# Unused products in TensorE's idle time, and an offset of its own for each group of operations: a window attention and two MLPs on one core

## The chip, the core and the metric

The kernel runs on one core of one Trainium2 chip. The core has TensorE (PE in the rows; PEld is its weight load), VectorE (DVE), ScalarE (ACT), GpSimd (POOL) and SyncE (SP, which only issues transfers here). Each engine works off its own instructions in the order in which they stand, and waits at the head of its queue until what an instruction needs is there. The metric is the device time in microseconds (us) of one execution.

## The reference

```python
def _attn_ref(q, k, v):                       # 4 batches, 8 heads, 576 positions, head size 64
    scores = scale * np.matmul(q, k.transpose(0, 1, 3, 2))
    rel = pos[:, None] - pos[None, :]
    bias = slopes[:, None, None] * (-np.abs(rel).astype(np.float32))[None, :, :]
    mask = (rel >= 0) & (rel < window)        # window = 128
    scores = np.where(mask, scores + bias[None], -1000000000.0)
    scores = scores - np.max(scores, axis=-1, keepdims=True)
    attn = np.exp(scores)
    attn = attn / (np.sum(attn, axis=-1, keepdims=True) + 1e-09)
    return np.matmul(attn, v).astype(np.float32)
...
def _moe_ref(x, w_in, w_out):                 # 2304 x 512, d_ff 2048
    h = x @ w_in
    sp = np.where(h > 20.0, h, np.log1p(np.exp(np.minimum(h, 20.0))))
    return ((h * np.tanh(sp)) @ w_out).astype(np.float32)
...
def _moe2_ref(x, w_in, w_out):
    h = x @ w_in
    g = np.where(h > 0.0, h, alpha * (np.exp(np.minimum(h, 0.0)) - 1.0))
    return (g @ w_out).astype(np.float32)
...
    x = np.ascontiguousarray(attn_out.transpose(0, 2, 1, 3)).reshape(B * S, H * D)
    x = _moe_ref(x=x, **moe_kwargs)
    return _moe2_ref(x=x, **moe2_kwargs)
```

So there is an attention in which each query sees itself and the 127 positions before it, then an MLP with the Mish function, then an MLP with ELU. The weights arrive as 64-bit numbers.

## The kernel before

**Products.** Large products run in a 32-bit format of reduced precision (fp32r). To keep accuracy each operand is split into a high and a low part (`xh`, `xl`; `wih`, `wil`; `woh`, `wol`; `gh`, `gl`), and each product is three: high by high, low by high, high by low.

**Weights.** Each of 32 blocks of a weight (16 blocks of `d_ff`, input and output side) goes through `load_weights`: a transfer into `raw`, one DVE operation (line 411), two ACT operations (414, 417), a DVE and a POOL operation (419, 422) that make the 32-bit number `bits`, a copy to the high part (353 on ACT or 354 on DVE) and a subtraction to the low part (363, DVE or POOL).

**Attention.** `unit` computes one pair of heads for one part of one batch: scores on PE (`ps_s`, lines 493 to 503), mask, bias and row minimum on DVE (514, 517), exp on ACT (521), division (537 on DVE, 539 on ACT), a transpose on PE (`ps_t`, 562), a masked copy `pt` (578, 353, 587), the product with `v` (`ps_o`, 613). The first attention (batch 0, eight units) comes first of all, since everything else needs its result or stands behind it.

**First MLP.** The positions are cut into chunks of 512 (one per batch) and one of the tails. `steps` is the list of the pieces of hidden products: chunk 0 in 16 steps of two blocks by 256 positions, the later chunks in 16 steps of one block by 512 positions (the tails: two blocks by 256). A step is `hidden1` (24 products of 256 columns, or 12 of 512, into the bank `ph`, line 702), Mish on ACT (709), the split into `gh` and `gl` (353 or 354, and 363), and two steps later `output1` (as many products into `py`, line 730). Steps are counted from 0 here, so step 12 has the 13th Mish. Mish and exp need different tables in ACT, so ACT loads a table (`ACT_TABLE_LOAD`) between attention and Mish. The result goes to DRAM (`ys`, `x_scratch`).

**Second MLP.** Five chunks by 16 steps: `hidden2` (`ph2`, line 843; 12 products of 512 columns), exp, minimum and maximum (851, 852, 854), the split (353, 363), `output2` (872).

**Banks.** PSUM is shared out as two banks each of `h` (`ph`, `ph2`), `y` and `z` (results) and `a` (attention). A hidden step can start only when the split of the step before the last one has read its bank: `gl` frees it.

**The order.** `Plan` collects all operations with their priority (a due time worked out from the numbers in `AT`), and `order()` plays them through with a cost for each: whenever an engine is free, the ready operation with the lowest priority number whose buffers have room is taken and put out next. A copy or a subtraction goes to whichever of two engines would be done with it first. So the numbers in `AT` decide what stands where on every engine. When PE finds nothing, before a planned 80 us and as long as no `z` bank was taken, an unused product is put out:

```python
                    if best is None:
                        if e == "pe" and self.fill and t < self.fill[2] and not self.rings["z"]["next"]:
                            out.append(self.fill[1])
```

It multiplies constant ones, 256 columns of bf16, into a `z` bank that nobody has taken (line 308), and its result is never read.

Of the kernel before, what the change touches and what calls it, by code (L numbers as in the profile page):

```python
# [33 lines left out]
class Buffer:  # L34


    def __init__(self, ring, seq, make):
        self.ring, self.seq, self.make = ring, seq, make
        self.ops, self.real, self.left, self.taken, self.free_at = 0, None, 0, False, None
# [7 lines left out]
class Plan:  # L47
# [6 lines left out]

    WARM = 6.9
# [6 lines left out]
    def __init__(self):  # L62
        self.ops, self.rings, self.last = [], {}, {}
        self.fill, self.early = None, []
# [19 lines left out]
    def op(self, ways, reads=(), writes=(), prio=0.0, moved=0, rows=1.0, table=None, port=False):  # L84
# [20 lines left out]
        self.ops.append(dict(ways=ways, deps=deps, bufs=bufs, prio=prio, moved=moved, rows=rows, table=table, port=port))  # L105

    def order(self):
# [47 lines left out]
        while events:  # L155
# [4 lines left out]
            while again:  # L160
                again = False
                for e, q in waiting.items():
# [26 lines left out]
                    for b in o["bufs"]:  # L189
                        if not b.taken:  # L190
                            b.taken = True
                            b.ring["next"] += 1
                    at = t
# [32 lines left out]
        return out  # L226

# [33 lines left out]
def tile_window_attention_two_mlps(ctx, tc, qkv0, qkv1, qkv2, w1d, w2d, out):  # L261
# [46 lines left out]
    plan.fill = (256 / 2400 + 0.003, lambda: nc.tensor.matmul(unused[:, :256], ones[:, :P], ones[:, :256], start=True, stop=True), AT["fill"])  # L308
# [10 lines left out]
    def buf(tag, shape, dt=F32, name=None):  # L319
# [4 lines left out]
        def make():  # L324
            t = where.tile([P, words], dt, tag=tag, name=name or tag, bufs=slots)
# [8 lines left out]
        x = plan.buffer(tag, slots, make)  # L334
        return x

# [62 lines left out]
    def load_weights(wd, into, f, k, pr, stage):  # L399

        hi, lo = (buf(nm, (DM,), F32R) for nm in (("wih", "wil"), ("woh", "wol"))[k])
        into[f, k] = hi, lo
        for o in range(0, DM, HW):
# [24 lines left out]
                lambda hi=hi, o=o: hi()[:, o:o + HW], [bits] + [(hi, x) for x in parts], [(lo, x) for x in parts], pr + AT["wlo"])  # L428

# [522 lines left out]
```

## Time and profile before

| what | value |
|---|---|
| median of 3 runs | 952.38 us (952.3 to 956.86) |
| time of the profiled execution | 954.04 us |
| span of the profiled execution, first to last instruction | 952.3 us |
| mean granted TensorE clock (1 is full speed) | 0.983 |
| busy: PE, DVE, ACT, POOL | 932.0, 514.6, 505.8, 175.1 us |

The profiler records each instruction's start and length. A busy time is the time in which at least one instruction of the engine runs. PE's lengths hold the whole way of a product through the array, so they overlap, and a busy PE is not PE at its peak. The granted clock is recorded beside it: 1.00 is 2.4 GHz and 0.50 is 1.2 GHz. A wait is put down to the instruction whose end released the waiting one.

### The profile page before, as it was taken

The page shows a single profiled execution, that of the slowest core. Times are in us where ns is not written, and L with a number is a line of the kernel's source. Part 1 is how long each engine was busy: PE and PEld are TensorE (multiplying, and loading weights), DVE is VectorE, ACT ScalarE, POOL GpSimd, SP SyncE. Part 2 cuts the span into 40 slices and gives each one's busy share as a digit, 9 for nine tenths or more (in the row PEclk, how much of TensorE's full clock was granted, in tenths as well). Part 3 has the DMA queues.
Part 4 walks back from the last instruction along what each step waited for, and adds up shares of the span by engine and source line. Part 5 has one row for each costly group of instructions (what it writes and reads, how often), then busy time and mean ns, then how long its engine had stood idle before and what let it go on. Part 6 is the DMA issues. An engine that isn't in the chain of part 4 may idle for free.

```text
span 952.3 us, 13731 instructions
## 1 busy us (share of the span) xinstructions
PE 932.0 (98%) x5061; PEld 775.9 (81%) x5061; DVE 514.6 (54%) x1305; ACT 505.8 (53%) x1022; POOL 175.1 (18%) x153
## 2 busy tenths in 40 slices
PE   9989998999999999999999999999999999999998
PEld 6668987978878777789988878888888888888887
DVE  7776878767623346871477796343334333333333
ACT  5788988785826566882477773233223222322232
POOL 2553454520100001010355552000000000000000
PEclk9789998999999999999999999999999999999999
DMA  8343445233212123440444541011001000100010
GB/s 237 118 134 114 158 156 179 91 121 107 77 35 70 42 59 103 131 138 34 124 157 141 166 154 34 1 45 45 1 0 41 27 1 1 44 1 1 1 45 23
DMA packets 32387, 75.08 MB, mean 79 GB/s; under 512 B 5696, under 2 KB 12352, under 8 KB 32320
## 3 DMA queue, kind: packets, MB, share of 16 engines
q1 hardware_dynamic: 32320, 74.20, 24.7%
q8 instruction: 40, 0.66, 0.3%
q14 instruction: 27, 0.22, 0.1%
HBM read 64.23 MB, written 9.96 MB: 78 GB/s over the span
## 4 chain that ended last, share of the span: by engine, by line
PE 79%; DVE 2%; ACT 1%; DMA 1%; issue 0%; DVEq 0%
PE py L872 21%; PE ph L843 20%; PE py L730 17%; PE ph L702 16%; PE ps_o L613 2%; PE ps_t L562 1%; PE ps_s L496 1%; PE ps_s L498 1%; PE ps_s L503 1%; DMA qkv<-in_qkv_dram 1%; DVE kk L363 0%; DMA x_scratch<-ys 0%; DVE ps_s L514 0%; DVE p L537 0%; DVE gl L363 0%
## 5 line engine op out<-in xcount | busy, mean ns | idle before, releaser
L363 DVE TENSOR_TENSOR gl<-ph,gh 128x512 fp32r<-128x512 f32 (+1 forms) x152 | 100.3, 660 | 168.7 <-ACT gh L353 168.2
L843 PE MATMUL ph<-x,wih 128*128 128x512 f32 (+1 forms) x640 | 181.8, 368 | 2.4 <-DVE gl L363 2.4
L353 ACT ACTIVATE gh<-ph 128x512 fp32r<-128x512 f32 (+1 forms) x143 | 81.6, 572 | 128.6 <-PE py L872 125.1
L843 PEld LDWEIGHTS ph<-x,wih 128*128 128x128 f32 x640 | 117.4, 188 | 25.4 <-DVE gl L363 3.1
L730 PE MATMUL py<-gh,woh 128*128 128x256 f32 (+1 forms) x384 | 136.2, 355 | 1.7 <-ACT gh L353 1.0
L702 PE MATMUL ph<-xh,wih 128*128 128x256 f32 (+1 forms) x384 | 134.5, 350 | 1.3 <-DVE gl L363 1.0
L730 PE MATMUL py<-gh,wol 128*128 128x256 f32 (+1 forms) x384 | 130.4, 340 | 1.0 <-DVE wol L363 0.6
L702 PE MATMUL ph<-xl,wih 128*128 128x256 f32 (+1 forms) x384 | 130.1, 339 | 0.7 <-DVE xl L363 0.7
L730 PE MATMUL py<-gl,woh 128*128 128x256 f32 (+1 forms) x384 | 130.3, 339 | 0.3 <-DVE gl L363 0.3
L702 PE MATMUL ph<-xh,wil 128*128 128x256 f32 (+1 forms) x384 | 130.0, 339 | 0.0
L843 PE MATMUL ph<-x,wil 128*128 128x512 f32 (+1 forms) x320 | 117.7, 368 | 0.0
L851 ACT ACTIVATE e<-ph 128x512 f32<-128x512 f32 (+1 forms) x80 | 44.4, 555 | 133.3 <-PE ph L843 132.4
L872 PE MATMUL py<-woh,gl 128*128 128x512 f32 x288 | 112.3, 390 | 0.0
L872 PE MATMUL py<-woh,gh 128*128 128x512 f32 x288 | 112.3, 390 | 0.0
L872 PE MATMUL py<-wol,gh 128*128 128x512 f32 x288 | 112.1, 389 | 0.0
L422 POOL TENSOR_TENSOR bits<-bits,raw 128x512 int32<-128x512 int32 x64 | 89.1, 1395 | 98.4 <-DVE bits L419 75.0
L852 DVE TENSOR_SCALAR e<-e 128x512 f32<-128x512 f32 (+1 forms) x80 | 34.7, 434 | 112.8 <-ACT e L851 112.5
L702 PEld LDWEIGHTS ph<-xh,wih 128*128 128x128 f32 x384 | 73.4, 191 | 13.0 <-issue 3.3
L730 PEld LDWEIGHTS py<-gh,woh 128*128 128x128 f32 x384 | 73.7, 192 | 10.9 <-issue 1.5
L730 PEld LDWEIGHTS py<-gh,wol 128*128 128x128 f32 x384 | 73.6, 192 | 9.6 <-DVE wol L363 1.0
L702 PEld LDWEIGHTS ph<-xh,wil 128*128 128x128 f32 x384 | 73.5, 192 | 7.8
L702 PEld LDWEIGHTS ph<-xl,wih 128*128 128x128 f32 x384 | 73.6, 192 | 7.6 <-DVE xl L363 0.9
(101 smaller groups left out, 1498.4 us busy)
## 6 DMA issues: line engine op xcount, KB each, us to landing
raw<-in_w_dram SPq DMA_DIRECT2D x64, 512.0 KB, 4.2
qkv<-in_qkv_dram SPq DMA_DIRECT2D x12, 640.0 KB, 4.0
qkv<-in_qkv_dram SPq DMA_DIRECT2D x16, 288.0 KB, 2.9
x_scratch<-ys SPq DMA_DIRECT2D x18, 256.0 KB, 2.2
out_dram<-yo SPq DMA_DIRECT2D x18, 256.0 KB, 2.0
qkv<-in_qkv_dram SPq DMA_DIRECT2D x8, 512.0 KB, 3.6
xr<-x_scratch SPq DMA_DIRECT2D x16, 256.0 KB, 2.8
v<-in_qkv_dram SPq DMA_DIRECT2D x12, 192.0 KB, 2.4
```

The source lines that it names most:

```text
L353: ways = [("act", act_cost(n, sbuf), lambda: nc.scalar.activation(o(), i(), AF.Copy), 0.0), ("dve", dve_cost(n, sbuf), lambda: nc.vector.t ...
L363: both(n, lambda eng: eng.tensor_tensor(out=o(), in0=i(), in1=hi().bitcast(F32), op=ALU.subtract), reads, writes, prio, only, port=not only)
L422: gps(HW, lambda raw=raw, bits=bits: nc.gpsimd.tensor_tensor(out=bits().bitcast(I32), in0=bits().bitcast(I32), in1=raw()[:, :, 0].bitcast( ...
L496: nc.tensor.matmul(o, qh()[:, j, qo:qo + r], kk()[:, j, ks], start=(j == 0), stop=False, skip_group_check=True)
L498: nc.tensor.matmul(o, ql()[:, j, qo:qo + r], kk()[:, j, ks], start=False, stop=True, skip_group_check=True)
L613: nc.tensor.matmul(o()[j * D:(j + 1) * D, c0:c0 + math.prod(y.shape[1:])], vn()[:kr, n, j], y, start=n == 0, stop=n == nkb - 1, skip_group ...
L702: nc.tensor.matmul(ph()[:, i * n:(i + 1) * n], wt()[:, cs], xx()[:, at], start=(c == 0 and m == 0), stop=(c == KC - 1 and m == 2))
L730: nc.tensor.matmul(py()[:, k, :], wt()[:, cs], gg()[:, i * n:(i + 1) * n], start=(f == 0 and a == 0 and k == 0), stop=(f == NF - 1 and a = ...
L843: nc.tensor.matmul(ph(), wt()[:, cs], xx(), start=(c == 0 and m == 0), stop=(c == KC - 1 and m == 2))
L851: act(n, lambda: nc.scalar.activation(e(), ph(), AF.Exp), [ph], [e], t, sbuf=False, table="exp")
L852: dve(n, lambda: nc.vector.tensor_scalar(out=e(), in0=e(), scalar1=1.0, scalar2=-1.0, op0=ALU.min, op1=ALU.add), (), [e], t, fast=True)
L872: nc.tensor.matmul(py(), gg()[:, ts_], wt(), start=(f == 0 and a == 0), stop=(f == NF - 1 and a == 2))
```

## The change

First, PE's idle time takes unused products for longer: up to a planned 170 us instead of 80, and once the `z` banks are in use they go into the bank that the next attention, hidden or output operation will take (`spare`, which names none while PE has lately been busy enough by the planner's own count). That operation starts its bank anew, so it overwrites them. Second, each operation belongs to a group (one step's hidden products, one unit's scores, one block of weights), and the dictionary `SHIFT` adds an offset to the priority of 114 such groups. Third, a few numbers of `AT` differ (`late`, `relt`, `wadd`, `fill`). The new numbers `k0`, `k1`, `u4` and `u5` stand at values that give the steps and start times of before, and the new form of `output1` and `split_x` gives the same products.

```diff
-AT = dict(lag=2, step=6.96, late=23.66, copy=1.19, both=0.34, conv=-34.61, conv1=8.2, mish=-3.26, out=-0.67,
+AT = dict(lag=2, step=6.96, late=25.76, copy=1.19, both=0.34, conv=-34.61, conv1=8.2, mish=-3.26, out=-0.67,
...
-          g=-8.44, stage=-21.52, fill=80.0, u0=0.0, u1=5.67, t0=1.26, t1=11.22, t2=4.45, u2=33.61, u3=4.87,
-          norma=0.5, normp=8.33, relt=-13.66, d00=-2.11, d01=-2.85, d10=0.27, d11=1.21, dx=3.28, plain=6.14,
-          mm2=8.39, first=-1000.0, second=-53.57, wadd=2.54, whi=-10.73, wlo=9.29, norm=-2.13, mask=-3.68, gl=13.52,
-          newton=-9.59, elu=-24.7, lead=1, turn=2.71, held=28.54)
+          g=-8.44, stage=-21.52, fill=170.0, enough=1.5, u0=0.0, u1=5.67, t0=1.26, t1=11.22, t2=4.45, u2=33.61, u3=4.87,
+          norma=0.5, normp=8.33, relt=-15.35, d00=-2.11, d01=-2.85, d10=0.27, d11=1.21, dx=3.28, plain=6.14,
+          mm2=8.39, first=-1000.0, second=-53.57, wadd=1.47, whi=-10.73, wlo=9.29, norm=-2.13, mask=-3.68, gl=13.52,
+          newton=-9.59, elu=-24.7, lead=1, turn=2.71, held=28.54, k0=8, k1=0, u4=0.0, u5=5.67)
+
+SHIFT = dict(H10=18, H11=60.7, H12=6.4, H13=-5.2, H18=-8, H2=-14.4, H4=5.8, H6=-28.2, H68=26.9, H69=44.6, H7=-24.9,
...
+    ENOUGH = AT["enough"]
...
-        self.ops.append(dict(ways=ways, deps=deps, bufs=bufs, prio=prio, moved=moved, rows=rows, table=table, port=port))
+        prio += SHIFT.get(self.group, 0.0)
+        self.ops.append(dict(group=self.group, ways=ways, deps=deps, bufs=bufs, prio=prio, moved=moved, rows=rows, table=table, port=port))
...
-                        if e == "pe" and self.fill and t < self.fill[2] and not self.rings["z"]["next"]:
+                        if e != "pe" or t > self.fill[2]:
+                            continue
+                        if t <= self.WARM or not self.rings["z"]["next"]:
                             out.append(self.fill[1])
-                            free[e] = self.clocked(t, self.fill[0], 1.0)
-                            heapq.heappush(events, free[e])
+                        else:
+                            b = self.spare(q, t)
+                            if b is None:
+                                continue
+                            b.taken = True
+                            b.ring["next"] += b.seq == b.ring["next"]
+                            out.append(lambda b=b: self.fill[3](b))
+                        free[e] = self.clocked(t, self.fill[0], 1.0)
+                        heapq.heappush(events, free[e])
                         continue
...
+    def spare(self, q, t):
+
+        k = int(t / self.TICK)
+        if self.columns.get(k, 0) + self.columns.get(k - 1, 0) * (k + 1 - t / self.TICK) > self.ENOUGH * self.COLUMNS:
+            return None
+        for i in sorted(q, key=lambda i: (self.ops[i]["prio"], i)):
+            bufs = self.ops[i]["bufs"]
+            if all(self.room(b, t) for b in bufs):
+                for b in bufs:
+                    if b.bank and (not b.taken or b.unused):
+                        b.unused = True
+                        return b
+        return None
...
+    unused_product = lambda to: nc.tensor.matmul(to[:, :256], ones[:, :P], ones[:, :256], start=True, stop=True)
+
+    def unused_before(b):
+        b()
+        unused_product(b.whole)
+
+    plan.fill = (256 / 2400 + 0.003, lambda: unused_product(unused), AT["fill"], unused_before)
```

The order of instructions on the engines shows what this moves. The rows below are instructions in the order in which they stand, without times; a number behind a name tells one buffer from another of the same name.

**PE in the first attention.** PE of before, behind the transpose of the third unit's probabilities; a row `LDWEIGHTS` and the `MATMUL unused` behind it are one unused product, and four of them stand here:

```order
L562 MATMUL ps_t_294<-ident_68,p_202 128x128 x2
L493 MATMUL ps_s_302<-qkv_153,qkv_146 128x256 x2
L562 MATMUL ps_t_318<-ident_68,p_257 128x128 x2
L308 LDWEIGHTS const-bfloat16-1.0
L308 MATMUL unused_67<-const-bfloat16-1.0 128x256
...
L493 MATMUL ps_s_336<-qkv_171,qkv_166 128x256 x2
L613 MATMUL ps_o_350<-pt_274,qkv_112 64x256 x2
```

PE of the change at the same place, where thirteen of them stand, and further on, where the first ones stand that go into the bank of a later product (four ahead of the product `ps_o_621`):

```order
L623 MATMUL ps_t_294<-ident_68,p_202 128x128 x2
L554 MATMUL ps_s_301<-qkv_153,qkv_146 128x256 x2
L623 MATMUL ps_t_316<-ident_68,p_202 128x128 x2
L623 MATMUL ps_t_322<-ident_68,p_253 128x128 x2
L351 LDWEIGHTS const-bfloat16-1.0
L351 MATMUL unused_67<-const-bfloat16-1.0 128x256
...
L623 MATMUL ps_t_356<-ident_68,p_253 128x128 x2
...
L351 MATMUL ps_o_621<-const-bfloat16-1.0 128x256
...
L623 MATMUL ps_t_632<-ident_68,p_536 128x128 x2
```

In all there are 82 unused products in place of 53: up to this place 44 in place of 41 (the 29 at the start among them), then 13 in place of 4, 8 in place of 8 before the first hidden products, and behind these 17 in place of none. The real products are the same 4720 in both.

**ACT around the 14th Mish.** ACT of before, from the 13th Mish (step 12, the first row) to the 14th (step 13, the last):

```order
L709 ACTIVATE ph<-ph 128x512
L353 ACTIVATE wih<-bits 128x512
L417 ACTIVATE raw<-raw 128x512
L353 ACTIVATE gh<-ph 128x512
L414 ACTIVATE raw<-raw 128x512
L709 ACTIVATE ph<-ph 128x512
```

ACT of the change between the same two, where 18 instructions and two table loads stand (left out are four of `raw`, one of `woh` and three of `p,st`):

```order
L777 ACTIVATE ph<-ph 128x512
L408 ACTIVATE woh<-bits 128x512
L408 ACTIVATE gh<-ph 128x512
L408 ACTIVATE wih<-bits 128x512
L582 ACT_TABLE_LOAD
L582 ACTIVATE p,st<-p,st 128x128
...
L473 ACTIVATE raw<-raw 128x512
L600 ACTIVATE p<-p,st 128x128 x4
L408 ACTIVATE wih<-bits 128x512
L777 ACT_TABLE_LOAD
L777 ACTIVATE ph<-ph 128x512
```

A unit's exp, four weight blocks' pieces and four divisions of the attention now stand between two steps that followed each other closely. The count of table loads is 71 in both.

**PE where the second MLP begins.** PE of before: half of the first `ph2`, then the last four groups of three `output1` products (`py`), then its other half, the second `ph2` and the third:

```order
L843 MATMUL ph2_5911<-x2_5135,wil_5151 128x512
L730 MATMUL py_5196<-gh_5895,woh_2279 128x512
...
L730 MATMUL py_5233<-gh_5895,wol_2298 128x512
L843 MATMUL ph2_5911<-x2_5155,wih_5137 128x512
...
L843 MATMUL ph2_5911<-x2_5181,wil_5151 128x512
L843 MATMUL ph2_5961<-x2_5125,wih_5190 128x512
...
L843 MATMUL ph2_5961<-x2_5181,wil_5201 128x512
L843 MATMUL ph2_6005<-x2_5125,wih_5248 128x512
```

PE of the change at the same place:

```order
L930 MATMUL ph2_5930<-x2_5154,wih_5166 128x512
...
L930 MATMUL ph2_5930<-x2_5210,wil_5180 128x512
L809 MATMUL py_5225<-gh_5940,woh_2340 128x512
...
L809 MATMUL py_5262<-gh_5940,wol_2351 128x512
L930 MATMUL ph2_5984<-x2_5154,wih_5219 128x512
...
L930 MATMUL ph2_5984<-x2_5210,wil_5230 128x512
L930 MATMUL ph2_6008<-x2_5154,wih_5277 128x512
```

All twelve products of the first `ph2` now stand ahead of the four `py` groups. On DVE two copies of `py` to `ys` stand ahead of the first `ph2`'s minimum where one stood (the other of the two was ACT's).

## Rows read from the trace of the kernel before

**Rows 1.** The page: span, busy time by engine, the clock in 40 slices

```profile
span 952.3 us, 13731 instructions
...
PE 932.0 (98%) x5061; PEld 775.9 (81%) x5061; DVE 514.6 (54%) x1305; ACT 505.8 (53%) x1022; POOL 175.1 (18%) x153
...
PEclk9789998999999999999999999999999999999999
```

**Rows 2.** Windows: PE, PEld, DVE, ACT, POOL busy, clock, DMA, GB/s

```profile
8.00:80.00 72.00, 65.46 (x378) 47.81 (x378) 56.13 (x206) 58.58 (x166) 33.58 (x41) 0.83 0.54 164
80.00:120.00 40.00, 39.81 (x319) 37.09 (x318) 30.70 (x80) 34.47 (x72) 16.85 (x12) 1.00 0.42 130
...
170.00:240.00 70.00, 69.39 (x426) 57.85 (x424) 51.53 (x159) 53.05 (x110) 20.07 (x14) 1.00 0.33 101
...
549.00:564.00 15.00, 12.64 (x56) 10.10 (x56) 13.74 (x17) 12.38 (x22) 9.69 (x8) 1.00 0.66 206
```

**Rows 3.** Windows, the same columns: the four stretches at half clock

```profile
19.30:29.50 10.20, 10.20 (x39) 5.71 (x38) 5.84 (x26) 5.87 (x22) 3.42 (x5) 0.50 0.82 273
43.20:53.40 10.20, 9.56 (x42) 7.19 (x41) 10.10 (x32) 8.99 (x23) 7.80 (x11) 0.50 0.42 135
70.50:73.90 3.40, 3.40 (x16) 2.47 (x17) 3.35 (x14) 3.39 (x11) 1.74 (x2) 0.50 0.60 204
155.80:162.70 6.90, 6.40 (x32) 5.21 (x32) 6.76 (x24) 6.61 (x17) 2.65 (x3) 0.51 0.61 203
```

**Rows 4.** Windows, the same columns: what stands just ahead of those

```profile
16.00:19.30 3.30, 2.18 (x12) 1.40 (x12) 2.32 (x13) 2.87 (x11) 0.75 (x2) 1.00 1.07 292
39.80:43.20 3.40, 2.02 (x10) 1.19 (x9) 2.63 (x12) 2.66 (x10) 1.09 (x2) 1.00 0.28 77
67.00:70.50 3.50, 2.05 (x10) 1.43 (x11) 2.34 (x7) 2.64 (x5) 1.14 (x2) 1.00 0.47 122
152.40:155.80 3.40, 1.25 (x8) 0.82 (x7) 3.37 (x10) 3.39 (x6) 2.51 (x2) 1.00 0.66 219
```

**Rows 5.** Windows of line L308 alone (PE, PEld): unused products

```profile
19.30:29.50 10.20, 2.10 (x8) 1.04 (x8) 0.50 0.82 273
```

**Rows 6.** Waits of PE, 8 to 240 us: three of 16 rows

```profile
PE ps_t L562 <- DVE p L537: 1.7, 2, 1.4
...
PE ps_s L493 <- DMA qkv<-in_qkv_dram: 0.8, 1, 0.8
...
PE ps_s L503 <- DVE st L517: 0.2, 1, 0.2
```

**Rows 7.** Windows, the columns of group 2

```profile
145.00:163.00 18.00, 14.29 (x93) 11.93 (x92) 17.25 (x51) 16.75 (x37) 6.76 (x6) 0.81 0.58 197
```

**Rows 8.** ACT's timeline around the 13th and 14th Mish (line L709)

```profile
152.07 1.28 ACT L709 ACT_TABLE_LOAD   x1
153.37 0.58 ACT L709 ACTIVATE ph<-ph 128x512 f32<-128x512 f32 x1
...
155.99 0.60 ACT L709 ACTIVATE ph<-ph 128x512 f32<-128x512 f32 x1
```

**Rows 9.** Instructions of ACT up to 240 us: busy, mean ns

```profile
L539 ACT ACTIVATE p<-p,st 128x128 f32<-128x128 f32 x20 | 6.9, 392 | 0.0
```

**Rows 10.** Chain in order of time: start, length, products

```profile
169.58 1.44 PE py L730 x12
...
886.37 3.40 PE py L872 x15
```

**Rows 11.** PE's timeline where the second MLP begins

```profile
554.71 0.39 PE L843 MATMUL ph<-x,wil 128*128 128x512 f32 x1
...
557.43 0.39 PE L843 MATMUL ph<-x,wil 128*128 128x512 f32 x1
560.18 0.73 PE L843 MATMUL ph<-x,wih 128*128 128x512 f32 x2 [2.36 <-DVE gl L363]
```

**Rows 12.** DVE's timeline at the same place

```profile
559.45 0.68 DVE L363 TENSOR_TENSOR gl<-ph,gh 128x512 fp32r<-128x512 f32 x1
```

More of the change, by code (lines that the diff above doesn't have):

```diff
@@ L38, in __init__ @@
         self.ring, self.seq, self.make = ring, seq, make
-        self.ops, self.real, self.left, self.taken, self.free_at = 0, None, 0, False, None
+        self.real, self.left, self.taken, self.free_at = None, 0, False, None
+        self.bank, self.unused = False, False
     def __call__(self):
@@ L192, in order @@
                             b.ring["next"] += 1
+                        b.unused = False
                     at = t
@@ L324, in make @@
         def make():
-            t = where.tile([P, words], dt, tag=tag, name=name or tag, bufs=slots)
+            t = x.whole = where.tile([P, words], dt, tag=tag, name=name or tag, bufs=slots)
             n = math.prod(shape)
@@ L334, in buf, with grouped @@
         x = plan.buffer(tag, slots, make)
+        x.bank = where is psum
         return x
+    def grouped(name, fn, *a):
+        plan.group = name
+        fn(*a)
+        plan.group = None
     def act(n, emit, reads, writes, prio, sbuf=True, extra=0, table=None):
@@ L442, in unit @@
         tp = t0 + AT["prep"] * dt
+        me = f"u{b}{part}{pr}"
+        plan.group = me + "l"
         cut = [sum(W[:i]) for i in range(4)]
@@ L666, in operands, with split_x @@
         x_of[ci] = [(buf(f"xh{c}", (C2,), F32R), buf(f"xl{c}", (C2,), F32R)) for c in range(KC)]
-    def split_x(ci, t):
-        need = [(b, 2) for b in range(B)] if ci == B else [(ci, 0), (ci, 1)]
+    def split_x(ci, t, only=None):
+        need = [(b, 2) for b in range(B)] if ci == B else [(ci, x) for x in range(2) if only in (None, x)]
         if any((*x, pr) not in ended for x in need for pr in range(NPAIR)):
@@ L673, in split_x @@
         parts = range(n // C1)
+        if only is not None:
+            parts, n = [only], C1
+        at = slice(parts[0] * C1, parts[0] * C1 + n)
         if ci == B:
@@ L716, in output1 @@
         n = C2 // len(fs)
-        if fs[0] == 0:
-            py_of[ci, half] = [buf(tag, (C2 // n, n), name="py") for tag in ("yyzz" if n == C2 else "zz" if half else "yy")]
-        ys_of = py_of[ci, half]
+        if (ci, half) not in py_of:
+            if ci in (0, B):
+                py_of[ci, half] = [(buf("yz"[half], (2, C1), name="py"), half, (2 * y, 2 * y + 1)) for y in range(2)]
+            else:
+                py_of[ci, 0] = py_of[ci, 1] = [(buf(tag, (1, C2), name="py"), None, (y,)) for y, tag in enumerate("yyzz")]
@@ L720, in output1, with mm @@
         gh, gl = g_of.pop(s)
+        targets = py_of[ci, half] if n == C1 else [x for h in range(2) if ci == 0 or not h for x in py_of[ci, h]]
         for i, f in enumerate(fs):
             woh, wol = w1[f, 1]
-            w = C2 // n
-            for y, py in enumerate(ys_of):
-                def mm(i=i, f=f, y=y, py=py, woh=woh, wol=wol):
-                    for k in range(w):
-                        cs = slice((w * y + k) * P, (w * y + k + 1) * P)
+            for y, (py, only, cols) in enumerate(targets):
+                g0 = i * n if n == C1 else C1 * (only or 0)
+                o0 = half * C1 if only is None else 0
+                m = C1 if n == C1 or only is not None else C2
+                first = (ci, py) not in begun
+                begun.add((ci, py))
+                def mm(f=f, py=py, woh=woh, wol=wol, cols=cols, g0=g0, o0=o0, m=m, first=first):
+                    for k, c in enumerate(cols):
+                        cs = slice(c * P, (c + 1) * P)
@@ L788, in tile_window_attention_two_mlps @@
             if fs[0] == 0 and ci > 0:
-                at(t - 0.2, split_x, ci, t + AT["split"])
+                at(t - 0.2, grouped, f"x{ci}{steps[s][2]}", split_x, ci, t + AT["split"], steps[s][2] if ci == 1 and K1 else None)
             at(t, hidden1, s, t)
```

74 lines of the change are left out of this document (53 added, 21 removed).

## The prediction

> **What bounds the kernel now.** I read the page first. PE is busy 932.0 of 952.3 us [rows 1], so the time is PE's work plus what PE loses to waits and to the lower clock, and only those losses can change: the real products are the same 4720. The clock line of the page shows where the lower clock lies: as a 7 or an 8 in three of the first seven slices, 0 to 167 us, and nowhere behind [rows 1]. The windows then cut the span by how PE does. From 80 to 120 us and from 170 to 240 us PE is busy 39.81 of 40 and 69.39 of 70 us at clock 1.00 [rows 2], so there nothing is lost. Losses are in 8 to 80 us (mean clock 0.83), around 145 to 163 us (clock 0.81, PE busy 14.29 of 18) [rows 2, 7], and 2.4 us of waiting in 549 to 564 us [rows 2].
>
> The windows at half clock say what the clock costs. PE is busy 10.20, 9.56, 3.40 and 6.40 us in them [rows 3]; at 1.2 GHz that is work of half the time, so 5.1, 4.8, 1.7 and 3.2 us are lost at most. What the reader is to see beside it is who else is full. In the first stretch DVE and ACT work 5.84 and 5.87 of 10.20 us: there everybody waits for PE. In the others DVE works 10.10 of 10.20, 3.35 of 3.40 and 6.76 of 6.90 us, and ACT nearly as much [rows 3]: there a faster PE would soon wait for them. Just ahead of each stretch PE was thinly busy: 2.18 of 3.30, 2.02 of 3.40, 2.05 of 3.50 and 1.25 of 3.40 us [rows 4]. The waits of PE are many and small: 16 rows that add up to 12.6 us, no single one over 1.4 us [rows 6].
>
> **The change, part by part.** The sum is made against the profiled span, 952.3 us. That execution took 954.04 us as a whole, 1.7 more; the median of the runs is 952.38, so the span and the median agree within 0.1 us, and I apply the sum to the median.
>
> *The unused products themselves.* There are 29 more. Eight of them take 2.10 us at half clock [rows 5], 0.26 each, so the added ones cost from nothing (if each lies in idle time of PE) to 7.6 us (if none does). The order puts thirteen where before has four behind the third unit's transpose, and the later ones ahead of attention products and hidden products near the places of [rows 4]; PE is idle 1.1 to 2.2 us in each of those windows. Thirteen at 0.13 (full clock) are 1.7 us against 1.1 idle there, so a little is not hidden: I take +0.5.
>
> *The first stretch at half clock.* Of its 10.20 busy us, 2.10 are unused products [rows 5], so real work is 8.1 us at half speed and 4.05 us could be won if the clock stayed up. DVE and ACT can follow, with 4.3 us idle each. The hole that stands ahead of it (1.12 us of 3.30) is what the thirteen products fill. It is not sure that the clock stays for all of it, since the same attention has few products per microsecond either way. From 0 to -4.0; I take two thirds, -2.7.
>
> *The second and third stretch.* Up to (9.56 + 3.40) / 2 = 6.5 us of PE's time, but DVE is full in both [rows 3], so nearly all of it would come back as waits for DVE or ACT. From 0 to -6.5; I take -1.0, near the lower end, since the row says that DVE has 0.15 us left of 13.6.
>
> *145 to 163 us.* PE is idle 18 - 14.29 = 3.7 us there [rows 7] and loses 3.2 to the clock, 6.9 in all, because DVE (17.25) and ACT (16.75) are full for all 18. They are much less full later (51.53 and 53.05 of 70 us from 170 to 240 us, [rows 2]), so it is a peak of work that can be moved. The order gives PE more to do meanwhile. Between the last hidden product of step 14 and the first output product that reads its result stand 52 products in before and 99 in the change; for step 15 it is 45 and 89, for step 16 29 and 67. They hold 24 hidden products of the next chunk, of 512 columns, which before has behind. At 0.12 us for 256 columns (1.44 for 12) and 0.227 for 512 (3.40 for 15) [rows 10], the cover of step 14 goes from about 6 to about 14 us. Against it stands ACT: see the rival below. From -6.9 to +4.7 (the rival's); I take -2.5.
>
> *More work on ACT.* Up to the 25th Mish the change puts on ACT five more divisions, three more copies out of `ps_o`, two more of weights, one more each of `q`, `kk` and `pt` and one fewer of `gh`, twelve more in all, which DVE did before. A division is 0.39 us [rows 9]; twelve such are 4.7 us. ACT works 34.47 of 40 us from 80 to 120 us [rows 2], so it has room, but not everywhere. From 0 to +4.7; I take +1.0.
>
> *The other waits.* Of the 12.6 us [rows 6] some 9 lie outside 145 to 163 us. The offsets shift all of them, in both directions. SP's transfers are the same, and some stand a few places earlier or later in its queue; of PE's waits 0.8 us end on a transfer [rows 6], so I price that move at nothing, at most 0.8 either way. From -4 to +2; I take -0.7.
>
> *Where the second MLP begins.* This one can be followed through. Before, the third `ph2` waits 2.36 us for the `gl` of the first [rows 11], since both use the same bank of `h`. The first one's last product starts at 554.71 and holds PE 0.23 us, so it ends at 554.94; `gl` ends at 559.45 + 0.68 = 560.13 [rows 11, 12]: the chain of exp, minimum, maximum and split takes 5.2 us, and PE has only the second `ph2` to put into it, 12 x 0.227 = 2.72 us. In the change the four `py` groups stand there too, another 12 x 0.227 = 2.72 us: 5.44 in all, so the chain fits. But one more copy to `ys` now stands on DVE ahead of it, and it has to wait for `py` products. I leave 0.6 of the wait: -1.8 (from -2.4 to 0).
>
> Sum: 0.5 - 2.7 - 1.0 - 2.5 + 1.0 - 0.7 - 1.8 = -7.2, so 952.4 - 7.2 = **945.2 us**.
>
> **The rivals.**
>
> *DVE and ACT set the pace.* The clock stays up, PE waits instead, and only the last term is left, 952.4 - 1.8 = 950.6 us. For it: in three of the four stretches DVE or ACT is full [rows 3], and the change takes no work from them together. Against it: the first stretch, where they are not. A second way to the same time is that the filling does not hold the clock at all. The page "TensorE: Matmul & The Clock Gate" of the Trainium skill, section "Part 1: The HAM clock gate", puts the lower clock down to an engine that sits idle, and says that the stretches at which the chip looks do not start with the kernel, so that the moment of a change moves from run to run. By the first half the filling of gaps as short as these would be worth nothing, and this trace disagrees: PE was busy for 2.02 of the 3.40 us ahead of a fall, with no single wait over 1.4 us [rows 4, 6]. By the second half products at fixed places would hold the clock in some runs and not in others; no run here shows that.
>
> *ACT's block of work ahead of the 14th Mish (slower).* Before, the 14th Mish starts 155.99 - 153.37 = 2.62 us behind the 13th, with four instructions between, 0.52 each [rows 8]. In the change 18 instructions and two table loads stand there: 8 attention ones at 0.39 [rows 9], 10 others and the 13th Mish itself at 0.52, two loads at 1.28 [rows 8], together 3.1 + 5.7 + 2.6 = 11.4 us. Then come the split on ACT and DVE (0.6 and 0.7 us), so step 13 frees its bank 13 us behind the start of the 13th Mish. Step 15 needs that bank, and between step 13's last and step 15's first hidden product PE has 58 products, some 7 us. If PE is through with step 13 by the time that the 13th Mish starts (as before, where ACT is late there), PE waits about 6 us, and half of a stretch like the last one at half clock, 3.2 us, comes on top: +9.2. With -2.7 and -1.8 from the other terms that is 952.4 + 4.7 = 957.1 us. It decides once step 13's products end more than some 6 us ahead of the 13th Mish's block. For it: ACT works 16.75 of 18 us there [rows 7]. Against it: the same step has 120 products between hidden and output.
>
> *All stretches go.* The clock stays up throughout, and DVE and ACT keep pace since the peak is spread: -4.0, -4.0 (of 6.5), -5.5 (of 6.9), -2.0, -2.4, with +1.5 for ACT and the fillers: -16.4, 936.0 us. For it: the fillers stand at the four places of [rows 4]. Against it: rows 3, where DVE is full.
>
> **How the numbers follow.** Forecast 0.45 (its own range 940 to 949 us), DVE and ACT set the pace 0.22 (949 to 954), ACT's block 0.17 (954 to 963), all stretches go 0.16 (932 to 940). The prediction is 945.2 us. The range 936 to 956 leaves out half of the last case and two thirds of the block's, 0.19 in all. What a measurement of this kernel can tell from no change is 0.5%, so faster means below 947.6 and slower above 957.1 us. Of the forecast 0.85 lies below 947.6, so faster is 0.16 + 0.38 = 0.54. Of the block's case some two thirds lie above 957.1, since its price stands at that bound and its spread goes up: slower 0.12. The rest, 0.34, is the same.
>
> **What would show it.** In the profile of the change: (1) no half clock between 19 and 30 us, and the first hidden products some 3 us earlier; (2) the wait of 2.4 us where the second MLP begins gone or under 1 us; (3) PE busy over 16 of the 18 us around the last steps of chunk 0 and no half clock there; (4) DVE and ACT as full as before from 40 to 60 us, so that PE waits there for them. Wrong would be: half clock at new places in the first 170 us, which would mean that the filling moved the thin stretches and did not remove them; or PE waiting several us for `gl` ahead of step 15.

## The result, and the profile after

The changed kernel takes 943.08 us (median of 4 runs, 942.03 to 944.11) against 952.68 us of the kernel before on the same chip: ratio 0.9889, 95% interval 0.986 to 0.9919. It is faster by 9.6 us, and the range of the prediction holds the time. In three of the experiments below one run of twelve took 965 to 967 us at a granted clock of 0.972 to 0.977, and the medians and ratios given for them leave it out. The profiled execution has a span of 942.4 us against 952.3.

The page of the changed kernel, in the lines of [rows 1]:

```profile
span 942.4 us, 13762 instructions
...
PE 924.6 (98%) x5090; PEld 773.2 (82%) x5090; DVE 512.3 (54%) x1304; ACT 506.0 (54%) x1031; POOL 164.7 (17%) x145
...
PEclk8999999999999999999999999999999999999999
```

PE is busy 7.4 us less, though it runs 29 products more. The clock line has one slice below 9 where before has three. The windows of the changed kernel (columns as in group 2): the two half-clock stretches that are left in the first 240 us, 40 to 60 us, the place of [rows 7], which comes some 5 us earlier now, and 8 to 240 us as a whole.

```profile
15.70:25.90 10.20, 9.64 (x38) 6.39 (x38) 6.00 (x35) 5.72 (x22) 2.18 (x3) 0.50 0.94 273
40.00:60.00 20.00, 15.58 (x102) 12.32 (x102) 18.41 (x49) 17.45 (x49) 12.79 (x16) 0.92 0.42 133
56.60:60.00 3.40, 3.40 (x19) 3.40 (x18) 2.28 (x4) 1.42 (x6) 1.22 (x1) 0.50 0.48 169
140.00:158.00 18.00, 16.61 (x137) 15.46 (x136) 16.04 (x43) 17.05 (x39) 8.72 (x7) 1.00 0.66 214
...
8.00:240.00 232.00, 219.21 (x1520) 186.50 (x1519) 179.79 (x556) 194.28 (x451) 84.56 (x77) 0.97 0.47 144
```

The same window of the kernel before, which was not shown ahead:

```profile
8.00:240.00 232.00, 218.85 (x1452) 182.83 (x1451) 180.27 (x550) 187.04 (x426) 92.13 (x82) 0.93 0.45 140
```

By these two rows PE's idle time from 8 to 240 us is 232 - 218.85 = 13.15 us before and 232 - 219.21 = 12.79 us after, nearly the same, and the clock is 0.93 against 0.97. Half clock lasts 10.2 + 10.2 + 3.4 + 6.9 = 30.7 us before [rows 3] and 10.2 + 3.4 = 13.6 us after, 17.1 us less, worth up to 8.5 us. But a busy PE of the change holds 29 more unused products, so idle time and clock alone do not say where the time was won. The count of products does. The window up to 145 us, first of before, then of the change with the one behind it (for before that one is [rows 7]); and the unused products among them (lines L308 and L351 alone), before and change:

```profile
8.00:145.00 137.00, 128.17 (x878) 106.50 (x878) 106.09 (x330) 112.50 (x272) 62.05 (x61) 0.91 0.49 153
```

```profile
8.00:145.00 137.00, 125.62 (x912) 106.54 (x911) 108.66 (x345) 118.91 (x294) 59.57 (x60) 0.95 0.52 159
145.00:163.00 18.00, 16.61 (x138) 15.07 (x138) 14.46 (x35) 17.31 (x36) 9.20 (x8) 1.00 0.56 184
```

```profile
8.00:145.00 137.00, 4.83 (x24) 2.34 (x24) 0.91 0.49 153
```

```profile
8.00:145.00 137.00, 9.15 (x52) 5.16 (x51) 0.95 0.52 159
```

Up to 145 us before has run 878 - 24 = 854 real products and the change 912 - 52 = 860: about the same, although the change has 10.2 us less of half clock up to there. That better clock had brought next to nothing: PE is idle for 11.38 us instead of 8.83, and more of its busy time is unused products. From 145 to 163 us before runs 93 products [rows 7] and the change 138, one of them unused. This is where most of the gain lies.

The waits of PE in the changed kernel, 8 to 240 us (answering to [rows 6]): total, times, longest.

```profile
PE ph L768 <- DVE gl L418: 5.0, 3, 2.2
PE ps_s L554 <- DVE st L578: 2.3, 1, 2.3
PE ps_t L623 <- ACT p L600: 1.6, 3, 0.9
...
PE ps_s L554 <- DMA qkv<-in_qkv_dram: 1.2, 3, 0.6
```

They are fewer and longer than before, with 2.3 us the longest instead of 1.4, and the seven rows of this view add up to 12.6 us like the 16 of before.

PE where the second MLP begins (answering to [rows 11]): the last product of the first `ph2` and the first one of the third; and DVE's `gl` of the first (answering to [rows 12]).

```profile
544.90 0.39 PE L930 MATMUL ph<-x,wil 128*128 128x512 f32 x1
...
550.57 0.62 PE L930 MATMUL ph<-x,wih 128*128 128x512 f32 x2
```

```profile
549.56 0.68 DVE L418 TENSOR_TENSOR gl<-ph,gh 128x512 fp32r<-128x512 f32 x1
```

The first `ph2` now ends ahead of the last four `py` groups, which take 2.72 us. Its last product would stand at 544.90 + 2.72 = 547.62 behind them, where before has 554.71: so 7.1 us are won up to here. `gl` ends at 550.24, and the third `ph2` starts at 550.57 without a wait, 9.6 us earlier than the 560.18 of before: 2.5 us more are won at this place. The last 0.3 us of the 9.9 us of span were not followed up.

### The profile page after: what moved, and what is told of

It reads as the page before. It is cut to its first block, busy times and chain, and to the rows that moved or that the text cites. A ratio compares the mean times of both kernels' runs of the same rounds, so it can differ in the third digit from the quotient of the medians.

```text
span 942.4 us, 13762 instructions
## 1 busy us (share of the span) xinstructions
PE 924.6 (98%) x5090; PEld 773.2 (82%) x5090; DVE 512.3 (54%) x1304; ACT 506.0 (54%) x1031; POOL 164.7 (17%) x145
## 4 chain that ended last, share of the span: by engine, by line
PE 89%; ACT 4%; DVE 4%; DMA 1%; issue 1%; SPq 1%; POOL 0%; ACTq 0%
PE ph L930 21%; PE py L962 21%; PE py L809 20%; PE ph L768 19%; PE ps_o L674 3%; PE ps_t L623 2%; DMA raw<-in_w_dram 1%; PE ps_s L554 1%; PE ps_s L557 1%; PE ps_s L559 1%; DVE bits L475 1%; SPq L505 1%; PE ps_s L564 1%; DVE bits L467 1%; ACT p L582 1%
```

## The experiments

All are run beside the kernel before, five rounds each. Four lots were run, and the kernel before has a median of 952.5 to 953.5 us in them. Theory one: **the order** that the offsets make brings the gain. Its rival: **the unused products** bring it, by holding the clock. Offsets are named by their group: H, g and O are the hidden products, the Mish with its split and the output products of a step, u the pieces of an attention unit (batch, part, pair), w and v the weights of the first and the second MLP.

**1. The unused products alone (e1_fill_only).**

```diff
-SHIFT = dict(H10=18, H11=60.7, ...
+SHIFT = {}
-late=25.76 ... relt=-15.35 ... wadd=1.47
+late=23.66 ... relt=-13.66 ... wadd=2.54
```

> The kernel before with the new unused products alone: no group has an offset, the three planner numbers are those of before, and idle time of TensorE up to 170 us takes products into the next bank (30 of them, and 53 into the first). If the gain comes from the order that the offsets make, this takes 950 to 954 us: the wait of 2.36 us at the second MLP stays, and the stretch from 145 to 163 us stays thin, since between the last hidden and the first output product of steps 14 and 15 there are 55 and 34 products, as few as before. If the gain comes from the unused products, which keep the clock up, it takes 945 to 948 us, and no half clock is left between 40 and 165 us.

Measured: ratio 1.0026 (1.0000 to 1.0052), a median of 956.86 us with eleven runs from 951 to 959 us. Without the offsets the products into later banks bring nothing. There are 53 into the first bank as before, so more of those in the order of before were not tried. (The profiled execution is the one of 966.87 us, so no row of it is read.)

**2. The offsets without unused products in later banks (e2_offsets_only).**

```diff
-                            b = self.spare(q, t)
+                            b = None
```

> The changed kernel without unused products in later banks: the offsets and the three numbers are there, and the 65 products into the first bank. If the gain comes from the order, this takes 942 to 945 us, with the covers of steps 14 and 15 at 100 and 90 products as in the change. If the unused products in later banks keep the clock, it takes 948 to 951 us: the half clock of before between 43 and 74 us and from 156 to 163 us is back, and only the 2.7 us at the second MLP and some at 200 us stay.

Measured: 942.50 us (940.95 to 945.33), ratio 0.9877 (0.9853 to 0.9901): the whole gain, without these products. Half clock between 43 and 74 us is back, as the rival has it, though not that from 156 to 163 us, and the time is no longer for it. Its longest stretch, and 8 to 240 us:

```profile
45.00:55.20 10.20, 9.65 (x45) 7.37 (x44) 7.65 (x22) 10.16 (x24) 7.88 (x10) 0.50 0.46 155
8.00:240.00 232.00, 221.60 (x1510) 188.62 (x1509) 177.22 (x558) 194.80 (x454) 86.70 (x78) 0.96 0.48 144
```

ACT is full in that stretch (10.16 of 10.20), so a faster PE would have had to wait for ACT. That half clock costs little where another engine is full, as the prediction's third term had it for DVE, fits this run: it has less full clock than the change (0.96 against 0.97), PE is idle for 10.4 us instead of 12.79, and the time is the same.

**3. The same order without the 17 products (e3_not_put_out).**

```diff
     def unused_before(b):
         b()
-        unused_product(b.whole)
```

> The changed kernel, in exactly its order on every engine, with the 17 unused products in later banks left out of the program (the bank is still taken early). This parts the products from the order that they led to. If the 17 products keep the clock, there is half clock again for 10 us or more between 40 and 170 us and the time is 946 to 951 us. If they do nothing by themselves, it is 942 to 944.5 us and the half-clock stretches are those of the change to one or two microseconds.

Measured: 943.79 us (943.56 to 947.06), ratio 0.9897 (0.9873 to 0.9921), the same as the change within the intervals. The window of 8 to 240 us is that of the change too:

```profile
8.00:240.00 232.00, 218.32 (x1506) 185.41 (x1506) 181.12 (x562) 194.48 (x452) 83.82 (x77) 0.97 0.47 144
```

**4. The same order with the 17 products three times (e10_three_times).**

```diff
-        unused_product(b.whole)
+        for _ in range(3):
+            unused_product(b.whole)
```

> The changed kernel in its own order, with each of the 17 unused products in later banks issued three times (51). If such products keep the clock, there is less half clock than with 17 and the time is 939 to 942 us. If they do nothing, it is 943 to 944 us where they lie in idle time, and up to 34 x 0.12 = 4 us more, 947 us, where they don't.

Measured: 944.05 us (942.59 to 945.16), ratio 0.9888 (0.9852 to 0.9924). PE is busy for 3.7 us more than in the change and the clock is again 0.97:

```profile
8.00:240.00 232.00, 222.88 (x1554) 188.98 (x1553) 178.92 (x554) 194.47 (x451) 84.50 (x77) 0.97 0.46 144
```

None, one and three of each take the same time within the intervals. The 17 products in later banks lie in idle time and do not hold the clock.

**5. The same order without any unused product in the first attention (e11_none_in_attention).**

```diff
-                            out.append(self.fill[1])
+                            out.append(self.fill[1] if t <= self.WARM else lambda: None)
...
-        unused_product(b.whole)
```

> The changed kernel in its own order, with no unused product after the first 29, which stand ahead of the first attention: 36 into the first bank and the 17 into later banks are left out. If unused products hold the clock anywhere, this has the most half clock between 15 and 100 us of all runs with this order, over 25 us, and takes 947 to 953 us. If they do not, it takes 941 to 944 us, since PE has 53 products less to do, many of them at half clock.

Measured: 953.57 us (952.81 to 955.93), ratio 0.9996 (0.9972 to 1.0020). The whole gain is lost. The clock falls at 10.4 us and stays down for 37.5 us:

```profile
10.40:47.90 37.50, 34.33 (x113) 20.87 (x113) 20.80 (x99) 22.55 (x79) 11.25 (x16) 0.50 0.56 156
```

So unused products do hold the clock, but it is those into the first bank, from 8 to 32 us. The kernel before has 24 of these and the change 36. The offsets need them: with none, the order is worth nothing.

**6. The same order without the thirteen (e12_without_thirteen).**

```diff
-                            out.append(self.fill[1])
+                            self.nth = getattr(self, "nth", 0) + (t > self.WARM)
+                            out.append(self.fill[1] if not 15 < self.nth <= 28 else lambda: None)
```

> The changed kernel in its own order, with the thirteen unused products behind the third unit's transpose left out (before has four there). The other 23 of the first attention and the 17 in later banks stay. In the profile of the change the thirteen stand at 22.4 to 25.0 us, inside the first half-clock stretch, which ends at 25.9 us; with none of the 36 in the first attention the clock stayed down until 47.9 us and the time was 953.6 us. If the thirteen are what brings the clock back, the first stretch lasts to 30 us or more and the time is 946 to 951 us. If it is the first fifteen or the last eight that hold the clock, the time is 941.5 to 944 us, since PE has 13 products less at half clock.

Measured: 945.86 us (942.61 to 947.69), ratio 0.9921 (0.9898 to 0.9944), 2.8 us above the change, though the two intervals overlap; every run but one has a granted clock of 0.986 to 0.988, where the change has 0.992 to 0.994. The first stretch lasts 17.0 us in the place of 10.2:

```profile
17.50:34.50 17.00, 16.57 (x56) 10.10 (x56) 10.38 (x48) 11.30 (x44) 6.29 (x9) 0.50 0.70 221
```

The thirteen end the stretch; they do not keep it from beginning. With the 23 that are left, about as many as the 24 of before, the order still has a ratio of 0.9921. So most of the gain does not need more unused products than before.

**7. Output products not put later (e4_out_not_late).**

```diff
-O12=43, O13=45, O15=122.6, O18=21.8, O20=4.4
```

> The changed kernel without the offsets of five groups of output products (O12, O13, O15, O18, O20), which the change puts later. Between the last hidden and the first output product of step 15 there are then 34 products in the place of 90, and for step 18 there are 35 in the place of 103. If the 6 us that the change wins between 145 and 163 us come from output products that are held back, so that hidden products of the next chunk stand in front of them, the time is 947 to 950 us, PE is busy under 15.5 of those 18 us again, and a half-clock stretch is back there. If they come from elsewhere (the attention's offsets, or the unused products), it stays at 942 to 945 us.

Measured: 945.66 us (944.56 to 948.85), ratio 0.9915 (0.9890 to 0.9939). It lies 2.6 us above the change (the intervals overlap), but not for the reason expected: the window that was to be thin again is not.

```profile
140.00:158.00 18.00, 16.60 (x136) 15.46 (x136) 16.07 (x41) 17.04 (x40) 8.25 (x7) 1.00 0.67 224
...
180.00:220.00 40.00, 39.22 (x216) 32.26 (x216) 26.38 (x88) 26.11 (x55) 8.32 (x6) 1.00 0.38 117
```

With 34 products of cover for step 15 in the place of 90, PE is as busy as in the change and the clock is as full. What is lost lies elsewhere, 0.8 us of it as idle time between 180 and 220 us, where the change has none.

**8. Without the offsets of the second attention (e5_no_second_attention).**

```diff
-u0200 u0211 u1000 u1001 u1010 u1011 u1013 u1021 u1023 u1024 u1033 u1034 u103f
-u1100 u1110 u1111 u1120 u1121 u112c u1131 x10
```

> The changed kernel without the 21 offsets of the attention of batch 1, of the first tail and of its split (u1..., u02..., x10). The covers of steps 14 and 15 stay long (117 and 128 products). If the 6 us between 145 and 163 us come from where DVE and ACT put the work of this second attention, the time is 947 to 951 us and PE waits there for several microseconds again, for gl or for p. If they come from the first attention's offsets or from the three numbers, by way of an earlier start of what follows, it stays at 942 to 945 us.

Measured: 961.75 us (960.7 to 963.29), ratio 1.0084 (1.0051 to 1.0116): worse than expected by either theory, and worse than before. The largest wait of PE, 100 to 200 us:

```profile
PE py L807 <- ACT woh L406: 6.5, 2, 3.3
```

The output products, delayed or not, now meet weights (`woh`) that ACT has not yet made.

**9. The offsets of the second attention alone (e7_second_attention_only).**

```diff
 on the kernel before:
+u0200=-2.5 u0211=-87.9 u1000=10.3 ... u1131=4.3 x10=104    (the 21 above)
```

> The kernel before with the 21 offsets of the attention of batch 1, of the first tail and of its split alone, with no further unused products and with its three numbers. The covers of steps 14 and 15 are 57 and 58 products, about as before. If the place of this work on DVE and ACT is what makes the 6 us, the time is 945 to 948 us. If the offsets work only together, it is 950 to 956 us: this work moves, and the rest of the order does not fit it.

Measured: a median of 955.35 us, ratio 1.0018 (0.9989 to 1.0046). By themselves they bring nothing. The clock is better than before, and PE waits instead, 17.9 us against 13.15:

```profile
8.00:240.00 232.00, 214.07 (x1454) 179.30 (x1454) 178.08 (x532) 185.95 (x439) 96.79 (x85) 0.96 0.45 140
```

**10. The offsets of the first attention alone (e8_first_only).**

```diff
 on the kernel before:
+late=25.76  relt=-15.35  wadd=1.47
+H2 H4 H6 H7 H9 O3 O5 O8 g0 g2 g8, all u00 and u01, w0 to w9    (41 groups)
```

> The kernel before with the three new numbers and the 41 offsets of the first attention, of steps 0 to 9 and of the first ten pairs of weights alone, without unused products in later banks. By the ledger of the two traces the change gains nothing up to 145 us, so if offsets act where they stand, this takes 950 to 954 us. But its order has already 100 and 88 products of cover for steps 14 and 15; if an earlier or smoother start is what spares PE the stop at 150 to 163 us, the time is 944 to 948 us.

Measured: 951.32 us (947.92 to 954.0), ratio 0.9978 (0.9950 to 1.0007). It has 100 and 88 products of cover for steps 14 and 15, like the change, and no measurable gain: a second blow to the reason that the prediction gave for 145 to 163 us. The balance is that of the run ahead, with 15.9 us idle:

```profile
8.00:240.00 232.00, 216.11 (x1476) 183.22 (x1476) 183.38 (x535) 194.58 (x458) 91.10 (x80) 0.96 0.45 141
```

**11. One Mish earlier (e9_one_mish).**

```diff
 on the kernel before:
+g12=-32.1
```

> The kernel before with one offset of the change alone: g12, so that the Mish of step 12 (the 13th Mish) stands earlier on ACT. Before, 18 instructions with five exps and two table loads stand between the 12th and the 13th Mish, and the 13th starts 7.0 us behind the last product that it waits for; here 10 stand there, and 17 with four exps come between the 13th and the 14th. If the late 13th Mish is what stops PE at 152 to 158 us, it starts some 4 us earlier, PE has the bank of step 14 in time, and the time is 947 to 950 us. If the work that is pushed behind it stops PE later instead (a block of ACT's ahead of the 14th Mish), it is 952 to 957 us.

Measured: a median of 956.53 us, ratio 1.0035 (1.0004 to 1.0066). The 13th Mish does start earlier, at 147.29 us instead of 153.37 [rows 8], and PE stops all the same. ACT's timeline, PE's at the same place, and two windows, that of [rows 7] and 8 to 240 us:

```profile
147.29 0.58 ACT L765 ACTIVATE ph<-ph 128x512 f32<-128x512 f32 x1
...
157.75 0.58 ACT L765 ACTIVATE ph<-ph 128x512 f32<-128x512 f32 x1
```

```profile
154.23 1.02 PE L611 MATMUL ps_t<-ident,p 128*128 128x128 f32 x4 [1.97 <-ACT p L588]
```

```profile
145.00:163.00 18.00, 13.78 (x85) 11.16 (x84) 15.33 (x42) 17.87 (x39) 6.87 (x6) 0.81 0.51 180
...
8.00:240.00 232.00, 213.23 (x1430) 178.07 (x1429) 175.85 (x528) 187.04 (x434) 89.37 (x80) 0.96 0.44 140
```

ACT works 17.87 of 18 us. What was late ahead of the 13th Mish is late behind it: PE waits for the division of `p`, and the 14th Mish starts 1.8 us later than before. From 8 to 240 us PE is idle for 18.8 us.

What tells 11 from 7 and the change is one number: the hidden products that PE runs between 147.0 and 157.9 us. The windows are those of the line of `ph` alone, PE and PEld, first of the kernel before, then of the change, then of the kernels of 7 and 11:

```profile
147.00:157.90 10.90, 0.04 (x1) 0.02 (x1) 0.91 0.50 167
```

```profile
147.00:157.90 10.90, 5.06 (x36) 4.58 (x36) 1.00 0.78 251
```

```profile
147.00:157.90 10.90, 5.06 (x36) 4.58 (x36) 1.00 0.81 258
```

```profile
147.00:157.90 10.90, 0.00 (x0) 0.00 (x0) 0.90 0.48 165
```

Before, steps 12 and 13 are both through on PE at 147 us, both banks of `h` wait for a Mish, and PE has no hidden product to run for 10.9 us. In the change the 36 products are the 24 of step 13 and half of step 14. DVE's `gl` of steps 11 and 12, whose ends free the banks of steps 13 and 14, first of before, then of the change; then the `gl` of step 12 in the kernel of 11 and, on PE, the first hidden product behind it:

```profile
140.33 0.69 DVE L363 TENSOR_TENSOR gl<-ph,gh 128x512 fp32r<-128x512 f32 x1 [0.68 <-ACT gh L353]
157.08 0.68 DVE L363 TENSOR_TENSOR gl<-ph,gh 128x512 fp32r<-128x512 f32 x1
```

```profile
147.17 0.68 DVE L418 TENSOR_TENSOR gl<-ph,gh 128x512 fp32r<-128x512 f32 x1
148.43 0.68 DVE L418 TENSOR_TENSOR gl<-ph,gh 128x512 fp32r<-128x512 f32 x1
```

```profile
149.79 0.68 DVE L406 TENSOR_TENSOR gl<-ph,gh 128x512 fp32r<-128x512 f32 x1
```

```profile
160.08 0.58 PE L756 MATMUL ph<-xh,wih 128*128 128x256 f32 x1
```

The bank of step 13 comes free 6.8 us later than before, so its products are still there when PE needs work, and that of step 14 comes free 8.7 us earlier, behind the earlier 13th Mish. The kernel of 7 keeps both without the longer cover of step 15. In that of 11 the bank of step 14 is free at 150.47 us, early enough, but on PE the step stands behind the attention's transpose that waits for `p`, and it starts 9.6 us later: there the place in PE's order is missing and not the bank. The kernels of 9 and 10 have 12 and 18 hidden products in these 10.9 us and no gain. All this is counted from the traces; no run changes the two banks alone.

**12. Without the late offsets (e6_no_late).**

```diff
-H68 H69 H70 H71 O69 g68 g69 e3 I4 I5 P1 P2 P13 P29 v8_1 v12_1 v13_0 v15_0
```

> The changed kernel without the 18 offsets that act from 450 us on (H68 to H71, O69, g68, g69, e3, I4, I5, the P and the v). The order up to there is that of the change. If the 2.4 us wait of the third ph2 is all that these buy, the wait is back and the time is 943.1 + 2.4 = 945.5 us, at most 2.8 more with what stands around it. If the wait went for another reason (the weights of the first MLP, or the three numbers), the time stays at 943 us and no wait is there.

Measured: 945.95 us (943.72 to 948.72), ratio 0.9909 (0.9878 to 0.9940), 2.9 us above the change (the intervals overlap). PE's timeline has the old wait back, to the digit:

```profile
552.50 0.73 PE L928 MATMUL ph<-x,wih 128*128 128x512 f32 x2 [2.36 <-DVE gl L416]
```

**Did the order win by the clock?** The runs of the kernel before say how much the clock can do. Its 75 runs in the four lots have a granted clock from 0.979 to 0.996 and take 959.8 to 947.1 us. The ten at 0.992 or more have a median of 947.5 us, the nineteen at 0.982 or less one of 957.05 us. The change's four runs lie at 0.992 to 0.994 and take 943.08. So against runs of before with as good a clock it wins 947.5 - 943.1 = 4.4 us, of which some 2.5 to 2.9 are the second MLP; the other 5.2 us would then be that it has this clock in each of its four runs, and the kernel before in ten of 75. Four runs are few: the kernel of 3, which has the same order, had 0.985 to 0.993. And the mean clock does not say all: the kernel of 2 takes 942.5 us at a median clock of 0.9895, where before has 952.4 (31 runs at 0.989 to 0.991), so it matters which work the half clock falls on. One profile of each, that of before from a run at 0.983, can't settle that split further.

## Why the prediction was right, step by step

The sum was right by 2 us, and in part by luck: its first three terms, 0.5 - 2.7 - 1.0 = -3.2 us, belong to the time up to 145 us, where the change won next to nothing, and for 145 to 163 us it had -2.5 us, where the change won about 5.5. These two errors of 3 us cancel. The two profiled executions show 7.1 us up to where the second MLP begins and 2.5 us there.

*The unused products themselves (+0.5).* About nothing for the 17: with none, one and three of each the time is 943.8, 943.1 and 944.1 us. What the twelve further ones into the first bank cost by themselves no run shows.

*The first stretch (-2.7).* This step failed. The stretch did not go, it came earlier: 15.7 to 25.9 us instead of 19.3 to 29.5, behind a new wait of PE for `st` of 2.3 us. The thirteen were taken to fill the hole ahead of the stretch; they came too late for that and stand inside it, at its end. The prediction's sign (1) was wrong with it, in both halves: the first hidden product stands at 32.24 us instead of 30.29, later and not 3 us earlier. The thirteen are worth some 2.8 us (run 6), but as the end of the stretch, which is as long as before.

*The second and third stretch (-1.0).* Of 13.6 us, 3.4 are left. From 40 to 60 us DVE is busy 18.41 of 20 us, PE only 15.58, with one wait of 2.2 us for `gl` at 55.9 us: PE waits there for the others, as sign (4) said. The 10.2 us of half clock that went here had come to next to nothing by 145 us, even less than the -1.0.

*145 to 163 us (-2.5).* The gain came at this place, and its size was too small in the sum: PE busy 16.61 of 18 us and no half clock, sign (3). That is 16.61 - 14.29 = 2.3 us less idle and 3.2 [rows 7] less of clock, 5.5 in all. The reason given was wrong. Not the cover between hidden and output products did it: run 7 took that of step 15 away and lost nothing here, run 10 had the cover and won nothing. The cover does not even lie there: step 14 holds hidden products 337 to 360, and only 342 have run by 163 us before and 348 by 158 us in the change, so what stands behind its last one comes later. What PE got is hidden products inside the peak, by the count under run 11.

*More work on ACT (+1.0), other waits (-0.7).* ACT does more up to 240 us, 194.28 us against 187.04, so 7.2 us where the sum had 4.7, and as much less later, since the whole is 506.0 against 505.8. No wait can be put to this alone. PE's waits from 8 to 240 us add up to 12.6 us in both kernels.

*Where the second MLP begins (-1.8).* Right in each step, and 0.7 us too small. The order gives 550.57 - (544.90 + 0.23) = 5.44 us of work, as counted, and the chain to the end of `gl` takes 550.24 - 545.13 = 5.1 us, so the chain fits. The 0.6 us left for a copy on DVE were not needed.

*DVE and ACT set the pace.* This is what the change itself does up to 145 us, where the better clock brought no more products, and what the parts of the change do throughout. Runs 9, 10 and 11 have a clock of 0.96 from 8 to 240 us against 0.93, and take none of it home: PE is idle 17.9, 15.9 and 18.8 us. The whole set has the better clock at an idle time of 12.79 us. As for the second way, by the page "TensorE: Matmul & The Clock Gate" of the Trainium skill, section "Part 1: The HAM clock gate": its second half, that the moment of a change moves from run to run, fits the 75 runs of one program at 0.979 to 0.996. Its first half, the lower clock as that of an idle engine, does not fit the profile's busy time: in run 5 PE is recorded busy for 34.33 of 37.50 us at half clock, and there the fillers did pay.

*ACT's block ahead of the 14th Mish.* The block came, and was as long as priced. ACT's timeline of the changed kernel:

```profile
145.24 1.28 ACT L777 ACT_TABLE_LOAD   x1
146.53 0.58 ACT L777 ACTIVATE ph<-ph 128x512 f32<-128x512 f32 x1
...
158.70 0.58 ACT L777 ACTIVATE ph<-ph 128x512 f32<-128x512 f32 x1
```

12.2 us lie between the two (11.4 predicted). But the 13th Mish stands 6.8 us earlier than before, PE is only half through with step 13 when it starts, and so the point from which this rival decides is not reached. In run 11, where step 13 is through by then, PE does stop, but for another reason (`p`, 1.97 us, and not `gl` ahead of step 15), and the run is some 4 us above before and not 9.2.

*All stretches go.* No: 13.6 us of half clock are left.

## What to carry to other kernels

A table of offsets that was tuned as a whole is not a sum of small gains: parts of it alone (runs 9 to 11) were worth nothing, and one part taken out (run 8) cost 18.7 us. When PE starves while ACT and DVE are full, look at which buffers hold finished work that waits for them: before, two banks that were full at once left PE without a hidden product for 10.9 us. Weigh a kernel whose clock moves by many runs. And where unused products count as busy time, compare the real products that are done by a given time: here a better clock up to 145 us looked like the gain and had brought next to nothing.

## What the runs showed of the hardware

The same program ran with a mean granted clock from 0.979 to 0.996 and took from 959.8 to 947.1 us: a spread of 1.3% that goes with the clock, wider than the gain of the change. And without the unused products of the first attention (run 5) the clock stayed at 1.2 GHz from 10.4 to 47.9 us although PE was busy for 34.33 of these 37.50 us.
